# Later units' loads on ACT's queue, one-op state updates and a merged gather, in a two-layer attention kernel

## The chip, the cores and the metric

The kernel runs on one core of a Trainium2 chip. The metric is device time in microseconds (us) of one execution, the median of three runs.

## The reference

Gated linear attention over 4 batches x 8 heads, 768 tokens, head dimension 48, and behind it two feed-forward layers on the 3072 x 384 result, all in float32:

```python
state = np.zeros((B, H, D, D))
for t in range(S):
    state = alpha[:, :, t, :, None] * state + np.einsum('bhd,bhe->bhde', k[:, :, t], v[:, :, t])
    y[:, :, t] = np.einsum('bhd,bhde->bhe', q[:, :, t], state)
x = y.transpose(0, 2, 1, 3).reshape(B * S, H * D)
...
h = x @ w_in;  x = np.maximum(0.01 * h, h) @ w_out
h = x @ w2_in; out = np.where(h > 0, h, np.exp(np.minimum(h, 0)) - 1) @ w2_out
```

384 -> 2048 -> 384 in both layers. The weights are stored as 64-bit floats.

## The kernel before

**Engines.** PE is the matrix engine (TensorE), DVE the vector engine, ACT the scalar engine, POOL the general one, SP the engine that only starts transfers. A tile scheduler decides the order of the instructions on each engine and places the waits; the code gives it the order in which the steps are written. Each engine works through its own list in order. A transfer is started from the list of the engine that issues it, and that engine stops there until the transfer's conditions hold (its buffer is free; the transfer before it on the same of eight completion counters has landed).

**Attention.** The 3072 tokens are cut into 24 units of 128 tokens with all 8 heads, six units for each batch. Heads go in pairs: 112 partitions hold head 0 of a pair on 0 to 47 and head 1 on 64 to 111. For unit u, `load_unit` brings a "pack" (alpha, k and q, L113, three buffers) and `load_v` brings vt (L118, three buffers). `attn_prep` scans the decay products on DVE (E L130, F L134) and scales k and q (L136, L137). `attn_S` makes the scores sc (L149) and the transposed keys pk (L154) on PE; `attn_S_post` masks the scores into A (DVE, L161), copies pk to kn (ACT, L164) and multiplies the state S by the unit's decay into T (DVE, L169). `attn_V` adds A-by-values (L181) and T-by-queries (L186) in PSUM (po), and makes pu, the state's increment (L193). `attn_V_post` splits po into a rounded part xh (ACT, L202) and a rest xl (DVE, L203), and makes the new S = pu + T (DVE, L210; a copy in a batch's first unit, L212). T is one constant tile with zero blocks: for each head of a pair its own 48 of 96 columns are written, so T and S take one op for each half, and the matmul of L186 runs over all 112 rows.

**FFN1.** Four units make a block of 512 tokens; six blocks, each with 16 steps over 128 of the 2048 hidden columns. `gather` (L218) moves the 96 feature rows that do not fit the heads' layout with 12 transfers a block. A step is `ffn1_h` (hp, L259), `ffn1_g` (leaky ReLU, L267 on ACT and L268 on DVE; split into gh, L79 on ACT, and gl, L82 on DVE) and `ffn1_y` (L284), each product made of three passes (high x high, low x high, high x low). hp runs two steps ahead of y. The attention of block j+1 lies among the steps of block j. `next_load(u + 3)` is called at the end of unit u (L400).

**Weights.** `stage1(m)` loads step m's weights as 64-bit words into one of four slots (L418 to L420), and ACT and DVE turn them into a high and a low part (L232, L233, L241 on ACT; L237, L238, L240, L244 on DVE). This goes on during the attention of the first four units and block 0. The second layer's weights are converted the same way in FFN1's last block, from slots that `fill2` loads (L434).

**FFN2.** Six blocks of 512 tokens with 16 steps each: L313, then L320 and L321 on ACT, L322 on DVE, L79 and L82, then L344. A guard loads each unit's alpha again (span, L491) and checks its range with two ACT passes (L495, L496). It is written at every other step from block 1 on (L668).

Of the kernel before, what the change touches and what calls it, by code (L numbers as in the profile page):

```python
# [19 lines left out]
def attention_two_layers_kernel(  # L20
# [40 lines left out]

    ident = const.tile([128, 128], F32, name="ident")
    causal = const.tile([128, C], F32, name="causal")
    T = const.tile([PR, NP, PD], F32, name="T")
    d0 = const.tile([PR, EXT], F32, name="d0")
    d1 = const.tile([PR, EXT], F32, name="d1")
    bias = const.tile([PR, 2], F32, name="bias")
# [17 lines left out]
    def constants():  # L85
        make_identity(nc, ident)
        nc.gpsimd.memset(causal, 1.0)
        nc.gpsimd.affine_select(
            out=causal, in_=causal, compare_op=ALU.is_ge, fill=0.0,
            base=0, pattern=[[1, C]], channel_multiplier=-1,  # L90
        )
        nc.gpsimd.memset(T, 0.0)
        nc.vector.memset(d0, 0.0)
        nc.vector.memset(d0[:, 0:EXT:C + 1], 1.0)
        nc.vector.memset(d1, 0.0)
        nc.vector.memset(bias[:, 0:1], -1.0)
        nc.vector.memset(bias[:, 1:2], -ALPHA_SPAN)
        nc.vector.memset(far_sum[:, 1:2], 1.0)
# [3 lines left out]
    vts = {}  # L102
    st = {}

    def load_unit(u, first=False):
        t = pack_p.tile([PR, EXT + 2 * NP * C], F32, tag="pack", name="pack")
        if first:
            m = EXT + NP * C
            nc.sync.dma_start(t[:, 0:EXT], seqs[u, :, 0:EXT])
            nc.scalar.dma_start(t[:, EXT:m], seqs[u, :, EXT:m])  # L110
            nc.sync.dma_start(t[:, m:], seqs[u, :, m:])
        else:
            nc.sync.dma_start(t, seqs[u])  # L113
        packs[u] = t

    def load_v(u):
        t = v_p.tile([128, NP, 3 * D], F32, tag="v", name="vt")
        nc.sync.dma_start(t.rearrange("s p e -> s (p e)"), vals[u])  # L118
        vts[u] = t

    def ext(t, off):
# [35 lines left out]
    def attn_S_post(u):  # L157
        c = u % NC
        d = st[u]
        for j, sc in enumerate(d.pop("sc")):  # L160
            nc.vector.tensor_mul(d["A"][:, j], sc, causal.unsqueeze(1).to_broadcast([128, NP, C]))  # L161
        if c < NC - 1:
            kn = at_p.tile([128, NP, PR], F32, tag="kn", name="kn")
            nc.scalar.copy(kn, d.pop("pk"))  # L164
            d["kn"] = kn
        if c > 0:
            for j in range(2):
                r = slice(64 * j, 64 * j + D)
                nc.vector.tensor_mul(  # L169
                    T[r, :, j * D:(j + 1) * D], st["S"][r], d["pe"][r].to_broadcast([D, NP, D]))  # L170

    def attn_V(u):
        c = u % NC
        d = st[u]
        vt = vts.pop(u)
        A, qh = d["A"], d["qh"]
        po = ps_a.tile([PR, NP, C], F32, tag="at", name="po")
        for p in range(NP):
            for j in range(2):
                wide = D if j else 64  # L180
                nc.tensor.matmul(po[64 * j:64 * j + wide, p], lhsT=vt[:, p, 2 * j * D:2 * j * D + wide], rhs=A[:, j, p],  # L181
                                 start=(p == 0), stop=(p == NP - 1 and c == 0), skip_group_check=True)
        if c > 0:
            for p in range(NP):
                for j in range(2):
                    nc.tensor.matmul(po[64 * j:64 * j + D, p], lhsT=T[:, p, j * D:(j + 1) * D], rhs=qh[:, p],  # L186
                                     start=False, stop=(p == NP - 1), skip_group_check=True)
        d["po"] = po
        if c < NC - 1:
            pu = ps_a.tile([PR, NP, D], F32, tag="at", name="pu")  # L190
            for p in range(NP):
                for j in range(2):
                    nc.tensor.matmul(pu[64 * j:64 * j + D, p], lhsT=d["kn"][:, p, 64 * j:64 * j + D],  # L193
                                     rhs=vt[:, p, 2 * j * D:(2 * j + 1) * D], start=(p == 0), stop=(p == NP - 1),
                                     skip_group_check=True)
            d["pu"] = pu

    def attn_V_post(u, xh, xl, off):
        c = u % NC
        d = st.pop(u)  # L200
        po = d["po"]
        nc.scalar.copy(xh[0:PR, :, off:off + C], po)  # L202
        nc.vector.tensor_sub(xl[0:PR, :, off:off + C], po, xh[0:PR, :, off:off + C].bitcast(F32))  # L203
        if c < NC - 1:
            pu = d["pu"]
            Sn = at_p.tile([PR, NP, D], F32, tag="S", name="S")
            for j in range(2):
                r = slice(64 * j, 64 * j + D)
                if c > 0:
                    nc.vector.tensor_add(Sn[r], pu[r], T[r, :, j * D:(j + 1) * D])  # L210
                else:
                    nc.vector.tensor_copy(Sn[r], pu[r])  # L212
            st["S"] = Sn

    def gather(x, n):
        for b in range(2 * KD):
            lo, hi = 64 * (b // 3) + 16 * (b % 3), 64 * (b % 2) + D
            nc.sync.dma_start(x[hi:hi + 16, b // 2, :n].bitcast(F32), x[lo:lo + 16, KD, :n].bitcast(F32))  # L218


    w_words = [w1.bitcast(I32), w2.bitcast(I32)]
# [28 lines left out]
    steps = {}  # L250

    def ffn1_h(j, m):
        xh, xl, n = xt[j]
        hp = ps_h.tile([128, n], F32, tag="h", name="hp")
        wh, wl = win[m]
        i = 0
# [38 lines left out]
                    nc.scalar.copy(dst[:, c], ytiles[j][c])  # L295

    def x2_split(j):
        xh = xs_p.tile([128, KD, 512], F32R, tag="xh", name="xh")
        xl = xs_p.tile([128, KD, 512], F32R, tag="xl", name="xl")
        for c in range(KD):  # L300
            split(xh[:, c], xl[:, c], x2t[j][:, c], nc.scalar)
        x2s[j] = xh, xl
# [68 lines left out]
    def xtile(j):  # L371
        if j not in xt:
            n = blocks[j][1] * C
            xt[j] = (
                xs_p.tile([128, KD + 1, 512], F32R, tag="xh", name="xh"),
                xs_p.tile([128, KD + 1, 512], F32R, tag="xl", name="xl"),
                n,
            )
        return xt[j]

    def attn_pe(u, i):
# [5 lines left out]
    def attn_post(u, i):  # L387
# [4 lines left out]
                attn_prep(u + 1)  # L392
        elif i == 2:
            j = unit_block[u]
            xh, xl, _ = xtile(j)
            attn_V_post(u, xh, xl, (u - blocks[j][0]) * C)
            if u == blocks[j][0] + blocks[j][1] - 1:
                for x in (xh, xl):
                    gather(x, blocks[j][1] * C)
            next_load(u + 3)  # L400

    def next_load(u):
        if u < NU:
            load_unit(u)
            load_v(u)
        else:
            t = pack_p.tile([128, 2 * 768], I32, tag="pack", name="stg")
            slots2.extend([(t[:, 0:768], 99), (t[:, 768:1536], 99)])
# [95 lines left out]
    def general():  # L504
# [51 lines left out]
        weights(1)  # L556
        for j in range(NB):
            xt.pop(j)
            xh, xl, n = xtile(j)
            for i in range(n // C):  # L560
                r0 = blocks[j][0] * C + i * C
                xr = at_p.tile([128, KD, 128], F32, tag="A", name="xr")
# [18 lines left out]
    with ExitStack():  # L581
# [47 lines left out]
        for s, e in enumerate(seq):  # L629
# [35 lines left out]
                    conv2.b(2 * KF)  # L665
            if ph == 2 and m == 4 and (j + 1) * 512 < NT:
                x2_split(j + 1)
            if ph == 2 and j > 0:  # L668
                u, odd = divmod(after - 2 * KF, 2)
                if u <= NU and not odd:  # L670
                    if u < NU:
                        guard_load(u)
                    if u > 0:
                        guard_unit(u - 1)
                if u == NU + 1 and not odd:
                    guard()
        with tc.If(nc.values_load(near, min_val=0, max_val=1) == 0):
            general()
# [84 lines left out]
```

## Time and profile before

| | us |
|---|---|
| three runs | 987.18 to 989.9, median 989.37 |
| the profiled execution | 987.68 |
| its span, first to last instruction | 986.0 |
| busy in the span: PE / DVE / ACT | 934.5 / 545.6 / 446.6 |
| mean granted PE clock | 0.979 of full speed |

The profile is one execution recorded by the hardware profiler. Its page gives busy time by engine and the span in 40 slices; views of the same trace give stretches, groups of instructions, waits (who waited, for whom, how long in total, how often, the longest) and the instructions in order of time. PEld is PE's weight load, which overlaps its matmuls; SPq and ACTq are the transfers started from SP's and ACT's lists.

### The profile page before, as it was taken

How to read it: one execution, taken by the hardware profiler on the slowest of the kernel's cores; microseconds unless marked ns; L12 is line 12 of the kernel's file. 1: busy time of each engine (PE TensorE's matmuls, PEld its weight loads, DVE VectorE, ACT ScalarE, POOL GpSimd, SP SyncE). 2: the span in 40 equal slices, each digit the busy share in tenths (PEclk: the TensorE clock that was granted, in tenths of full speed). 3: DMA queues.
4: the chain of work that ended last, by engine and by line, in shares of the span. 5: the costliest groups of instructions: out<-in, count | busy, mean ns of one | idle time of the engine just before them, and what ended most of it. 6: DMA issues, size and time to landing. Idle time of an engine off the chain costs nothing.

```text
span 986.0 us, 13236 instructions
## 1 busy us (share of the span) xinstructions
PE 934.5 (95%) x5234; PEld 790.4 (80%) x5234; DVE 545.6 (55%) x916; ACT 446.6 (45%) x783; POOL 1.4 (0%) x9
## 2 busy tenths in 40 slices
PE   4689979899999999999999999999999999999996
PEld 3567757688788788888878889989989989899996
DVE  6799998533657556555559993433433333433332
ACT  1245453332322322233458874574574674444442
POOL 0000000000000000000000000000000000000000
PEclk9779998899999999999999999999999999999999
DMA  9655571000211212211134310030110210000001
GB/s 238 161 173 163 149 184 61 13 1 19 68 51 42 57 41 81 55 44 49 49 96 145 112 49 1 4 105 1 53 55 1 78 30 1 33 1 1 32 1 37
DMA packets 25671, 62.40 MB, mean 63 GB/s; under 512 B 4512, under 2 KB 7584, under 8 KB 25600
## 3 DMA queue, kind: packets, MB, share of 16 engines
q1 hardware_dynamic: 25472, 61.24, 22.0%
q8 instruction: 43, 0.70, 0.3%
q10 hardware_dynamic: 128, 0.23, 0.1%
q14 instruction: 28, 0.23, 0.1%
HBM read 54.37 MB, written 4.72 MB: 60 GB/s over the span
## 4 chain that ended last, share of the span: by engine, by line
PE 80%; DMA 9%; DVE 6%; ACT 2%; SPq 1%; issue 1%; DVEq 0%; ACTq 0%
PE y L284 19%; PE hp L259 18%; PE hp L313 18%; PE o L344 9%; PE oa L344 9%; DMA pack<-in_seqs_dram 3%; DMA x2t<-in_w_dram 3%; PE sc L149 2%; PE po L181 2%; DMA span<-in_seqs_dram 2%; PE po L186 1%; DMA out_dram<-osb 1%; ACT span L496 1%; DVE A L161 1%; DVE x2t L240 1%
## 5 line engine op out<-in xcount | busy, mean ns | idle before, releaser
L82 DVE TENSOR_TENSOR gl<-t,gh 128x512 fp32r<-128x512 f32 x192 | 132.1, 690 | 130.5 <-ACT gh L79 118.9
L79 ACT CAST gh<-t 128x512 fp32r<-128x512 f32 x192 | 118.9, 620 | 170.9 <-PE y L284 60.9
L284 PE MATMUL y<-gh,w 128*128 128x512 f32 x576 | 172.9, 398 | 2.9 <-ACT gh L79 2.9
L259 PE MATMUL hp<-xh,w 128*128 128x512 f32 x576 | 155.1, 402 | 4.6 <-DVE t L268 2.4
L313 PE MATMUL hp<-xh,w 128*128 128x512 f32 x576 | 149.2, 394 | 1.2 <-DVE t L322 1.2
L322 DVE SCALAR_TENSOR_TENSOR t<-t,hp 128x512 f32<-128x512 f32 x96 | 66.0, 687 | 152.2 <-ACT t L321 152.2
L259 PEld LDWEIGHTS hp<-xh,w 128*128 128x128 f32 x576 | 108.8, 192 | 29.6 <-issue 3.2
L284 PEld LDWEIGHTS y<-gh,w 128*128 128x128 f32 x576 | 107.2, 190 | 26.9 <-ACT gh L79 3.7
L313 PEld LDWEIGHTS hp<-xh,w 128*128 128x128 f32 x576 | 106.5, 188 | 19.0 <-DVE t L322 2.2
L284 PE MATMUL y<-gl,w 128*128 128x512 f32 x288 | 105.2, 399 | 0.4 <-DVE gl L82 0.4
L320 ACT ACTIVATE t<-hp 128x512 f32<-128x512 f32 x96 | 57.0, 594 | 105.8 <-PE hp L313 105.7
L268 DVE TENSOR_TENSOR t<-t,hp 128x512 f32<-128x512 f32 x96 | 65.2, 681 | 59.3 <-ACT t L267 59.1
L344 PE MATMUL oa<-w,gh 128*128 128x384 f32 x384 | 96.3, 337 | 1.3 <-ACT gh L79 1.3
L267 ACT ACTIVATE t<-hp 128x512 f32<-128x512 f32 x96 | 56.4, 596 | 90.7 <-PE hp L259 90.5
L344 PE MATMUL o<-w,gh 128*128 128x384 f32 x384 | 95.1, 337 | 1.9 <-ACT gh L79 1.9
L259 PE MATMUL hp<-xl,w 128*128 128x512 f32 x288 | 83.4, 393 | 0.0
L313 PE MATMUL hp<-xl,w 128*128 128x512 f32 x288 | 81.9, 392 | 0.0
L344 PEld LDWEIGHTS o<-w,gh 128*128 128x128 f32 x384 | 70.5, 188 | 7.7 <-ACT gh L79 2.7
L344 PEld LDWEIGHTS oa<-w,gh 128*128 128x128 f32 x384 | 70.1, 188 | 4.5 <-ACT gh L79 1.7
L284 PEld LDWEIGHTS y<-gl,w 128*128 128x128 f32 x288 | 53.6, 189 | 13.6 <-DVE gl L82 1.3
L313 PEld LDWEIGHTS hp<-xl,w 128*128 128x128 f32 x288 | 54.1, 188 | 12.2
L259 PEld LDWEIGHTS hp<-xl,w 128*128 128x128 f32 x288 | 54.3, 189 | 11.7 <-issue 0.2
(94 smaller groups left out, 1005.6 us busy)
## 6 DMA issues: line engine op xcount, KB each, us to landing
pack<-in_seqs_dram SPq DMA_DIRECT2D x23, 674.2 KB, 5.6
stg<-in_w_dram SPq DMA_DIRECT2D x28, 384.0 KB, 3.1
x2t<-in_w_dram SPq DMA_DIRECT2D x20, 384.0 KB, 4.6
vt<-in_vals_dram SPq DMA_DIRECT2D x24, 288.0 KB, 5.1
span<-in_seqs_dram SPq DMA_DIRECT2D x24, 226.2 KB, 2.7
x2t<-in_w_dram SPq DMA_DIRECT2D x32, 144.0 KB, 4.5
out_dram<-osb SPq DMA_DIRECT2D x24, 192.0 KB, 2.2
x2t<-in_w_dram SPq DMA_DIRECT2D x32, 48.0 KB, 4.3
```

The costliest lines, as they stand in the source:

```text
L79: nc.scalar.copy(dst, src)
L82: (lo_engine or nc.vector).tensor_sub(lo, src, dst.bitcast(F32))
L149: nc.tensor.matmul(sc[j][:, p], lhsT=kS[r, p, :], rhs=qh[r, p, :], start=True, stop=True)
L181: nc.tensor.matmul(po[64 * j:64 * j + wide, p], lhsT=vt[:, p, 2 * j * D:2 * j * D + wide], rhs=A[:, j, p], start=(p == 0), stop=(p == NP - ...
L259: nc.tensor.matmul(hp, lhsT=a[:, kk, :], rhs=x[:, kk, :n], start=(i == 0), stop=(i == 3 * KD - 1))
L267: nc.scalar.activation(t, hp, ACTF.Copy, scale=0.01)
L268: nc.vector.tensor_max(t, t, hp)
L284: nc.tensor.matmul(ytiles[j][c], lhsT=a[:, c * 128:(c + 1) * 128], rhs=x, start=(m == 0 and i == 0), stop=(m == KF - 1 and i == 2),)
L313: nc.tensor.matmul(hp, lhsT=a[:, kk, :], rhs=x[:, kk, :], start=(i == 0), stop=(i == 3 * KD - 1))
L320: nc.scalar.activation(t, hp, ACTF.Relu, scale=-1.0)
L322: nc.vector.scalar_tensor_tensor(out=t, in0=t, scalar=-1.0, in1=hp, op0=ALU.add, op1=ALU.max)
L344: nc.tensor.matmul(otiles[j][i], lhsT=a[:, i * 128:(i + 1) * 128], rhs=x, start=(m == 0 and n == 0), stop=(m == KF - 1 and n == 2),)
```

## The change

Four things. T becomes a tile of each unit with one 48-column block per head, written by one op over all 112 partitions, and S likewise; the T matmul runs over a head's 48 rows; POOL's memset of T goes. xh and xl of a block become two halves of one tile, and the gather moves both with 6 transfers in place of 12. The loads of units 3 to 23 are issued from ACT's list in place of SP's. The guard takes five units in each of FFN2's blocks 0 to 4, from step 6 on.

```diff
-    T = const.tile([PR, NP, PD], F32, name="T")
...
-        nc.gpsimd.memset(T, 0.0)
...
-    def load_unit(u, first=False):
+    def load_unit(u, first=False, eng=None):
...
-            nc.sync.dma_start(t, seqs[u])
+            (eng or nc.sync).dma_start(t, seqs[u])
...
-    def load_v(u):
+    def load_v(u, eng=None):
...
-        nc.sync.dma_start(t.rearrange("s p e -> s (p e)"), vals[u])
+        (eng or nc.sync).dma_start(t.rearrange("s p e -> s (p e)"), vals[u])
...
         if c > 0:
-            for j in range(2):
-                r = slice(64 * j, 64 * j + D)
-                nc.vector.tensor_mul(
-                    T[r, :, j * D:(j + 1) * D], st["S"][r], d["pe"][r].to_broadcast([D, NP, D]))
+            T = at_p.tile([PR, NP, D], F32, tag="cT", name="T")
+            nc.vector.tensor_mul(T, st["S"], d["pe"].to_broadcast([PR, NP, D]))
+            d["T"] = T
...
-                    nc.tensor.matmul(po[64 * j:64 * j + D, p], lhsT=T[:, p, j * D:(j + 1) * D], rhs=qh[:, p],
+                    r = slice(64 * j, 64 * j + D)
+                    nc.tensor.matmul(po[r, p], lhsT=d["T"][r, p], rhs=qh[r, p],
                                      start=False, stop=(p == NP - 1), skip_group_check=True)
...
-                    nc.tensor.matmul(pu[64 * j:64 * j + D, p], lhsT=d["kn"][:, p, 64 * j:64 * j + D],
+                    r = slice(64 * j, 64 * j + (D if j else 64))
+                    nc.tensor.matmul(pu[r, p], lhsT=d["kn"][:, p, r],
...
-            for j in range(2):
-                r = slice(64 * j, 64 * j + D)
-                if c > 0:
-                    nc.vector.tensor_add(Sn[r], pu[r], T[r, :, j * D:(j + 1) * D])
-                else:
-                    nc.vector.tensor_copy(Sn[r], pu[r])
+            if c > 0:
+                nc.vector.tensor_add(Sn, pu, d["T"])
+            else:
+                nc.vector.tensor_copy(Sn, pu)
...
-            nc.sync.dma_start(x[hi:hi + 16, b // 2, :n].bitcast(F32), x[lo:lo + 16, KD, :n].bitcast(F32))
+            nc.sync.dma_start(x[hi:hi + 16, :, b // 2, :n].bitcast(F32), x[lo:lo + 16, :, KD, :n].bitcast(F32))
...
-                for x in (xh, xl):
-                    gather(x, blocks[j][1] * C)
+                gather(t, blocks[j][1] * C)
             next_load(u + 3)
...
-            load_unit(u)
-            load_v(u)
+            load_unit(u, eng=nc.scalar)
+            load_v(u, eng=nc.scalar)
...
-            if ph == 2 and j > 0:
-                u, odd = divmod(after - 2 * KF, 2)
-                if u <= NU and not odd:
-                    if u < NU:
-                        guard_load(u)
-                    if u > 0:
-                        guard_unit(u - 1)
-                if u == NU + 1 and not odd:
+            if ph == 2 and m >= KF - 10 and m % 2 == 0:
+                u = 5 * j + (m - KF + 10) // 2
+                if u < NU:
+                    guard_load(u)
+                if 0 < u <= NU:
+                    guard_unit(u - 1)
+                if u == NU:
                     guard()
```

The scheduler orders each engine's list anew. Three places follow, each before and after. (The changed file is shorter, so its line numbers are lower by up to 8; buffer numbers differ as well.)

ACT's list at the start of the program, before: stage words x2t, copies kn and xh of the first units, no transfer.

```order
L233 ACTIVATE x2t_135<-x2t_135 128x768
L164 COPY kn<-pk 128x448
L233 ACTIVATE x2t_136<-x2t_136 128x768
L202 CAST xh<-po 112x4x128
L233 ACTIVATE x2t_137<-x2t_137 128x768
L164 COPY kn<-pk 128x448
L233 ACTIVATE x2t_138<-x2t_138 128x768
```

The same place after:

```order
L230 ACTIVATE x2t_134<-x2t_134 128x768
L162 COPY kn<-pk 128x448
L111 DMA pack<-in_seqs_dram 112x1541
L230 ACTIVATE x2t_135<-x2t_135 128x768
L201 CAST x<-po 112x4x128
L116 DMA vt<-in_vals_dram 128x576
L162 COPY kn<-pk 128x448
L230 ACTIVATE x2t_136<-x2t_136 128x768
L230 ACTIVATE x2t_137<-x2t_137 128x768
L116 DMA vt<-in_vals_dram 128x576
```

The pack of unit 3 stands behind the first kn copy, its vt behind the first copy of po. In SP's list the two stood behind all loads of the first four weight steps.

DVE's list around the last layer-1 weight conversion (w_15), before:

```order
L82 TENSOR_TENSOR gl<-t,gh 128x512
L244 TENSOR_TENSOR w_15_134<-x2t_140,w_15_133 128x768
L244 TENSOR_TENSOR w_14_132<-x2t_139,w_14_131 128x768
L130 SCALAR_TENSOR_TENSOR E<-pack,d_97 112x517
L132 TENSOR_SCALAR pe<-E 112x4
L136 TENSOR_TENSOR pack<-pack,E 112x512
L133 RECIPROCAL d_98<-pe 112x4
L134 SCALAR_TENSOR_TENSOR F<-pack,d_98 112x516
L137 TENSOR_TENSOR pack<-pack,F 112x512
L203 TENSOR_TENSOR xl<-po,xh 112x4x128 x3
L268 TENSOR_TENSOR t<-t,hp 128x512
```

The same place after:

```order
L81 TENSOR_TENSOR gl<-t,gh 128x512
L241 TENSOR_TENSOR w_15_133<-x2t_139,w_15_132 128x768
L265 TENSOR_TENSOR t<-t,hp 128x512
L81 TENSOR_TENSOR gl<-t,gh 128x512
L265 TENSOR_TENSOR t<-t,hp 128x512
L202 TENSOR_TENSOR x<-po,x 112x4x128 x2
L81 TENSOR_TENSOR gl<-t,gh 128x512
L265 TENSOR_TENSOR t<-t,hp 128x512
L81 TENSOR_TENSOR gl<-t,gh 128x512
L202 TENSOR_TENSOR x<-po,x 112x4x128
L265 TENSOR_TENSOR t<-t,hp 128x512
L128 SCALAR_TENSOR_TENSOR E<-pack,d_96 112x517
```

The three xl copies (x<-po after) stood behind the preparation of unit 13 (E to pack), and now stand ahead of it.

ACT's list in the first bunch of the guard, which begins FFN2's block 1, before; what lies between one gh cast (ahead of the first row) and the next:

```order
L495 ACTIVATE span<-span,bias 112x4x128
L496 ACTIVATE span,outside<-span,bias 112x4x128
L320 ACTIVATE t<-hp 128x512
L496 ACTIVATE span,outside<-span,bias 112x4x128
L495 ACTIVATE span<-span,bias 112x4x128
L321 ACTIVATE t<-t 128x512
L495 ACTIVATE span<-span,bias 112x4x128
L496 ACTIVATE span,outside<-span,bias 112x4x128
L320 ACTIVATE t<-hp 128x512
L495 ACTIVATE span<-span,bias 112x4x128
L496 ACTIVATE span,outside<-span,bias 112x4x128
L79 CAST gh<-t 128x512
```

After, the longest stretch between two gh casts in a bunch:

```order
L78 CAST gh<-t 128x512
L488 ACTIVATE span<-span,bias 112x4x128
L489 ACTIVATE span,outside<-span,bias 112x4x128
L488 ACTIVATE span<-span,bias 112x4x128
L317 ACTIVATE t<-hp 128x512
L489 ACTIVATE span,outside<-span,bias 112x4x128 x2
L318 ACTIVATE t<-t 128x512
L488 ACTIVATE span<-span,bias 112x4x128
L317 ACTIVATE t<-hp 128x512
L489 ACTIVATE span,outside<-span,bias 112x4x128
L78 CAST gh<-t 128x512
```

The guard's bunches had 8 units and stood at the start of blocks 1 to 3; now they have 5, at the starts of blocks 1 to 4 and one in block 0 beside the last weight conversions. (L495 and L496 became L488 and L489; L320 and L321 became L317 and L318.)

## Rows read from the trace of the kernel before

**Rows 1.** Stretches: length; busy us of PE, PEld, DVE, ACT, POOL; clock; DMA share; GB/s

```profile
0.00:25.00 25.00, 10.89 (x74) 8.63 (x74) 16.63 (x32) 4.21 (x6) 1.45 (x9) 1.00 0.95 238
30.00:167.00 137.00, 117.33 (x805) 90.41 (x805) 130.01 (x209) 58.80 (x87) 0.00 (x0) 0.89 0.52 144
200.00:250.00 50.00, 50.00 (x240) 41.24 (x239) 16.56 (x24) 15.21 (x25) 0.00 (x0) 1.00 0.09 22
646.00:714.00 68.00, 66.72 (x334) 59.95 (x333) 24.59 (x37) 41.09 (x77) 0.00 (x0) 1.00 0.13 38
850.00:918.00 68.00, 68.00 (x344) 61.50 (x343) 23.19 (x35) 31.15 (x52) 0.00 (x0) 1.00 0.04 12
```

**Rows 2.** Waits of DVE, 30 to 170 us (us in total, times, longest)

```profile
DVE E L130 <- DMA pack<-in_seqs_dram: 6.7, 3, 4.7
```

**Rows 3.** Waits of PE, 30 to 170 us

```profile
PE sc L149 <- DVE S L210: 3.2, 1, 3.2
...
PE hp L259 <- DMA xh<-xh: 2.1, 1, 2.1
```

**Rows 4.** DVE's groups by shape, 0 to 170 us (busy us, mean ns | idle before)

```profile
L161 DVE TENSOR_TENSOR A<-sc,causal 128x512 f32<-128x512 f32 x22 | 14.7, 680 | 0.0
...
L169 DVE TENSOR_TENSOR T<-S,pe 48x192 f32<-48x192 f32 x18 | 6.2, 347 | 0.3
...
L210 DVE TENSOR_TENSOR S<-pu,T 48x192 f32<-48x192 f32 x14 | 4.8, 346 | 1.0 <-PE pu L193 0.8
```

**Rows 5.** Timeline (start, us, instruction, idle before), 14 to 38 us, four engines

```profile
14.83 0.52 ACT L164 COPY kn<-pk 128x448 f32<-128x448 f32 x1
...
22.79 0.34 SPq L113 DMA_DIRECT2D pack<-in_seqs_dram  x1
...
29.94 0.90 ACT L232 ACTIVATE x2t<-x2t 128x768 f32<-128x768 f32 x1
...
30.46 1.24 DVE L130 TENSOR_TENSOR_SCAN E<-pack,d 112x517 f32<-112x517 f32 x1 [4.74 <-DMA pack<-in_seqs_dram]
...
37.55 0.96 DVE L238 SCALAR_TENSOR_TENSOR x2t<-x2t 128x768 int32<-128x768 int32 x1
```

**Rows 6.** The page's part 6: loads by line, KB each, us to landing

```profile
pack<-in_seqs_dram SPq DMA_DIRECT2D x23, 674.2 KB, 5.6
...
vt<-in_vals_dram SPq DMA_DIRECT2D x24, 288.0 KB, 5.1
```

**Rows 7.** Timeline, 171 to 177 us, DVE and PE

```profile
171.38 1.23 DVE L130 TENSOR_TENSOR_SCAN E<-pack,d 112x517 f32<-112x517 f32 x1 [4.26 <-DMA pack<-in_seqs_dram]
...
176.15 0.56 PE L193 MATMUL pu<-vt,kn 128*48 128x48 f32 x16 [2.88 <-DVE xl L203]
```

**Rows 8.** Waits of PE, 500 to 986 us

```profile
PE o L344 <- ACT gh L79: 1.9, 2, 1.0
PE hp L259 <- DVE t L268: 1.5, 1, 1.5
PE oa L344 <- ACT gh L79: 1.3, 1, 1.3
PE hp L313 <- DVE t L322: 1.2, 2, 0.8
```

**Rows 9.** Timeline, 269 to 271 us, ACT and SP's queue

```profile
269.67 0.58 ACT L202 CAST xh<-po 112x512 fp32r<-112x512 f32 x1 [1.65 <-PE po L181]
...
270.02 0.35 SPq L118 DMA_DIRECT2D vt<-in_vals_dram  x1
```

**Rows 10.** Stretch 200 to 300 us, PE's passes of L149, then of L186

```profile
200.00:300.00 100.00, 4.23 (x44) 3.27 (x44) 1.00 0.12 34
...
200.00:300.00 100.00, 2.29 (x32) 2.00 (x32) 1.00 0.12 34
```

**Rows 11.** Timeline, 254 to 258 us, ACT and PE

```profile
254.13 0.62 ACT L79 CAST gh<-t 128x512 fp32r<-128x512 f32 x1 [4.51 <-DVE t L268]
...
257.59 0.39 PE L284 MATMUL y<-gh,w 128*128 128x512 f32 x1
```

More of the change, by code (lines that the diff above doesn't have):

```diff
@@ L252, in ffn1_h @@
     def ffn1_h(j, m):
-        xh, xl, n = xt[j]
+        xh, xl, n, _ = xt[j]
         hp = ps_h.tile([128, n], F32, tag="h", name="hp")
@@ L297, in x2_split @@
     def x2_split(j):
-        xh = xs_p.tile([128, KD, 512], F32R, tag="xh", name="xh")
-        xl = xs_p.tile([128, KD, 512], F32R, tag="xl", name="xl")
+        t = xs_p.tile([128, 2, KD + 1, 512], F32R, tag="x", name="x")
+        xh, xl = t[:, 0], t[:, 1]
         for c in range(KD):
@@ L373, in xtile @@
             n = blocks[j][1] * C
[L374 to L378, printed above, removed]
+            t = xs_p.tile([128, 2, KD + 1, 512], F32R, tag="x", name="x")
+            xt[j] = t[:, 0], t[:, 1], n, t
         return xt[j]
@@ L394, in attn_post @@
             j = unit_block[u]
-            xh, xl, _ = xtile(j)
+            xh, xl, _, t = xtile(j)
             attn_V_post(u, xh, xl, (u - blocks[j][0]) * C)
             if u == blocks[j][0] + blocks[j][1] - 1:
-                for x in (xh, xl):
-                    gather(x, blocks[j][1] * C)
+                gather(t, blocks[j][1] * C)
             next_load(u + 3)
@@ L558, in general @@
             xt.pop(j)
-            xh, xl, n = xtile(j)
+            xh, xl, n, _ = xtile(j)
             for i in range(n // C):
```

## The prediction

> **What bounds the kernel now.** I read the stretches first. From 200 us on TensorE (PE) is busy all the time, 50.00 of 50 us, and DVE's 16.6 and ACT's 15.2 us of work lie beside it [rows 1]. FFN2 reads the same where no guard runs (68.00 of 68) and loses 1.3 us in a stretch with one (66.72). So after 200 us a faster DVE is worth nothing; only PE's own idle time can go. Earlier it is the other way round: in the 137 us from 30 to 167 DVE is busy for 130.0, PE for 117.3 and ACT for 58.8 [rows 1]. What DVE waits for around it is above all a unit's pack, 6.7 us before the decay scan, L130 [rows 2]. PE waits there for what DVE makes, 3.2 us for one S [rows 3]. So the first 170 us are as long as DVE's list of work plus its few waits, the next 400 as long as PE's matmuls, and FFN2 as long as PE's matmuls plus the guard's stalls.
>
> The granted clock of the stretch from 30 to 167 us is 0.89 on average [rows 1], so a part of it ran at the 1.2 GHz level. DVE is the bound there, so I count nothing for it; and PE's 19.7 idle us are more than what I take from DVE below.
>
> The profiled execution took 987.68 us (span 986.0). The median of the three runs, 989.37, is 1.7 us above it; I sum against the former and add 1.7.
>
> **1. T and S as one op each.** Up to 170 us DVE runs 18 T ops of 347 ns and 14 S ops of 346, each on 48 partitions x 192 [rows 4], and 4 S copies, which I take to be as long. The change makes one of two. The new op spans 112 partitions, still with 192 elements each. The mask multiply on 128 partitions takes 680 ns for 512, 1.3 ns an element; T on 48 takes 1.8 [rows 4]: more partitions don't make an element dearer, so I take a merged op to be as long as one was. 18 fewer ops x 0.35 = **6.3 us** less of DVE, all where DVE is the bound. The old ops behind 170 us lie beside PE's work: nothing.
>
> **2. Unit 3's pack.** DVE stands still for 4.74 us up to 30.46, because SP issued this load only at 22.79, behind the stage loads of four weight steps; it landed 7.7 us later [rows 5]. In the new order it stands on ACT right behind the copy of unit 0's pk, which ended at 15.35 [rows 5]. With 7.7 us to land it is there at about 23, before DVE ran dry at 25.7, and the whole 4.74 would go. But its bytes are not free. In the first 25 us the transfers are busy 0.95 of the time at 238 GB/s [rows 1]; unit 3's pack and vt, 674 + 288 KB [rows 6], set what is behind them back by 962 / 238 = 4.0 us, and that is weights of steps 2 and 3, which ACT has to have before the scale (L232) at 29.94. That ends at 30.84, and DVE's L238 needs it at 37.55 [rows 5]: 6.7 us of room, 2.0 once DVE comes 4.7 earlier. So 4.0 − 2.0 = 2.0 come back as a wait for ACT. Bounds 0 to 4.7; I take **2.7**.
>
> Here a rule speaks against the change. The Trainium skill, "DMA: Bandwidth & Descriptors", section "Issuing engines are not separate DMA queues", says that transfers started by any engine run on the same 16 DMA engines and interleave, so that starting them from several engines saves only the sequencer's time. By it this term would be 0 and the sum 2.7 smaller. The share of 0.95 agrees with it; a load that sat in SP's list while DVE was idle speaks against it.
>
> **3. The other waits for packs** up to 170 us: 6.7 − 4.7 = 2.0 us [rows 2, 5]. Bounds 0 to 2.0, I take **1.0**.
>
> **4. Unit 13's pack.** In SP's list a stage load stands ahead of it. DVE waited 4.26 us for it until 171.38, with three xl copies queued behind its preparation, and PE stood 2.88 us until 176.15 for the last of these [rows 7]. PE is the bound by then, so only the 2.88 count. In the new order the xl copies stand ahead of that scan, and even a late load doesn't hold PE. Bounds 0 to 2.9, I take **2.9**.
>
> **5. The guard.** Its waits are all of PE's idle time in FFN2: 1.9 + 1.3 us for gh, 1.2 for t [rows 8], 4.4 in all, in three bunches of 8 units that the scheduler puts at the starts of blocks 1 to 3. Now there are five bunches of 5. Between two gh casts ACT had four first and four second guard passes in the bunch shown above, and has three and four now, so the delay of a gh shrinks by one pass, and each bunch ends earlier. I leave 0.4 us for each of five: 4.4 − 2.0, rounded to **2.5**. Bounds 0 to 4.4.
>
> **6. The gather.** Six issues instead of twelve, each carrying both parts. PE waits 2.1 us for the first [rows 3], where DVE's list is the bound anyway, and the first matmul of the pass after the last waits 1.5 for a t behind the splits on DVE [rows 8]. Bounds 0 to 1.5, I take **1.0**.
>
> **7. What the change adds.** 42 loads go onto ACT's list. The issue of one took SP 0.35 us [rows 9]; 15 us in all, on an engine that is idle for over half of every stretch but FFN2's [rows 1]. An issue also waits until its buffer is free. Behind unit 8's pu SP issued the vt load at 270.02 [rows 9]; the xh copy, behind which ACT would issue it, began at 269.67 and takes 0.58 us [rows 9], so there the wait is nothing. In PE's stretch the cost is hidden if gh has room for 2 x 0.35 us, and the least that I found between the end of a gh cast and its first matmul is 2.8 us (254.75 to 257.59) [rows 11]. Up to 167 us ACT feeds DVE's conversions: 11 units x 0.7 = 7.7 us of issue on an ACT that is busy 58.8 of 137 us [rows 1]. Bounds 0 to 7.7; I take **+2.5**, nearer to 0, since ACT is idle for more than half of the time. T·qh goes from 112 to 48 rows, with the same 48 weight columns and 128 moving ones: 16 passes in each of 20 units, 11 of which lie behind 170 us: 176 passes where PE is the bound. The nearest rows are its own, 2.29 / 32 = 72 ns each, and the scores' 48-row passes, 4.23 / 44 = 96 [rows 10]; from below, two halves of a pair side by side would save 36. Bounds −6.3 to +4.2 us. I take 0, since as many columns stream. POOL's memset of T lay beside the first loads: nothing.
>
> **Sum:** −6.3 − 2.7 − 1.0 − 2.9 − 2.5 − 1.0 + 2.5 = −13.9, so 973.8 for a profiled execution, and with 1.7 more **975.5 us** for the median.
>
> **Rivals.**
> *The start gives nothing.* ACT's list is in order: a pack load that waits there holds the conversions behind it, and weights come as much later as packs come earlier. What DVE saves in terms 1 to 3 it then waits away, the issues' 2.5 with it, and terms 4 to 6 remain, −6.4: 983 (981 to 986.4). For it: the share of 0.95, and ACT's scale only at 29.94. It is the skill's rule above with ACT's order on top. Against: 130 of 137 us busy, where a removed op must show. Chance 0.17.
> *Nothing measurable*, 986.4 to 992.3 (0.3% either way is about what a measurement of this kernel can tell from no change): the first rival, and the issues at their bound of 7.7 in place of 2.5. Chance 0.08.
> *Slower: the loads hold gh.* In PE's stretch an ACT that waits for pu holds the gh cast behind it, and y on PE needs that. If the new order puts pu a step of 4.1 us behind po, each of 13 units costs 4.1 + 0.7 − 2.8 = 2.0 us, 26 in all, and with the −13.9 the time is 1001. It decides from a wait of 2.1 us per unit on, and eats the whole gain at 3.2. For it: the scheduler is free to put pu later. Against: unit 8's rows. Chance 0.12.
> Forecast, 963 to 981: chance 0.63.
>
> **How the numbers follow.** All terms at their best give −6.3 − 4.7 − 2.0 − 2.9 − 4.4 − 1.5 = −21.8, 967.6, and 961 with all of the matmuls' 6.3; I stop at 963. Upwards the range takes in the first rival and what its bounds leave, to 988. It leaves out the slower rival and most of the unchanged case, some 2 in 10. Faster by over 0.3% holds the forecast and the first rival, 0.80; same 0.08; slower 0.12.
>
> **What would show it.** Right: T and S once per unit at about 350 ns; under 2 us of idle time before unit 3's scan; DVE's last layer-1 conversion done some 8 us before 167; no wait of pu for xl at 176; FFN2's waits for gh and t at 2 us or less. Wrong: ACT waiting over a microsecond in front of a load with gh behind it; PE waiting for gh between 200 and 500 us; DVE waiting for L232 or L241 before 167; a merged op near 700 ns; T·qh passes at 96 ns.

## The result and the profile after

The changed kernel takes 971.99 us (median of four runs, 971.32 to 973.39), the kernel before 988.58 (four runs, 987.18 to 989.9). The ratio is 0.9834 with a 95% interval of 0.9815 to 0.9853, some 16.4 us faster. The forecast was 975.5, within 963 to 988. Two single executions among the experiments took far longer than the others of their kernels, 1246.96 us of the kernel before and 1848.2 us (the profiled one) of the changed kernel with 12 transfers; the times and ratios below leave both out, and the second gives no rows.

| | before | after |
|---|---|---|
| profiled execution / its span, us | 987.68 / 986.0 | 971.32 / 969.6 |
| PE / DVE / ACT busy, us | 934.5 / 545.6 / 446.6 | 929.8 / 529.4 / 445.8 |
| mean granted clock | 0.979 | 0.987 |

The stretches of the changed kernel, answering to [rows 1] (length; busy us of PE, PEld, DVE, ACT, POOL; clock; DMA share; GB/s):

```profile
30.00:167.00 137.00, 122.31 (x832) 90.89 (x828) 120.49 (x188) 62.86 (x93) 0.00 (x0) 0.93 0.52 146
646.00:714.00 68.00, 68.00 (x343) 61.58 (x342) 25.08 (x38) 38.51 (x69) 0.00 (x0) 1.00 0.09 29
850.00:918.00 68.00, 68.00 (x344) 61.72 (x343) 23.06 (x34) 31.47 (x52) 0.00 (x0) 1.00 0.04 12
```

DVE is busy for 120.5 of the 137 us that had 130.0, PE for 122.3 against 117.3, and the stretch of FFN2 with a guard is as full as the one without. The forecast lay 3.5 us above the measured time, and the sections below show that the sum was better than its terms.

**The start.** The same instructions as in [rows 5], on ACT, its queue and DVE (start, us, instruction, idle before):

```profile
14.39 0.51 ACT L162 COPY kn<-pk 128x448 f32<-128x448 f32 x1
...
15.30 0.32 ACTq L111 DMA_DIRECT2D pack<-in_seqs_dram  x1
...
24.96 1.24 DVE L128 TENSOR_TENSOR_SCAN E<-pack,d 112x517 f32<-112x517 f32 x1 [0.22 <-DMA pack<-in_seqs_dram]
...
30.93 0.90 ACT L230 ACTIVATE x2t<-x2t 128x768 int32<-128x768 uint16 x1 [3.48 <-DMA x2t<-in_w_dram]
...
31.73 0.88 ACT L229 ACTIVATE x2t<-x2t 128x768 f32<-128x768 f32 x1
...
32.63 0.96 DVE L235 SCALAR_TENSOR_TENSOR x2t<-x2t 128x768 int32<-128x768 int32 x1 [2.51 <-ACT x2t L229]
```

Unit 3's pack is issued at 15.30 in place of 22.79, and its scan waits 0.22 us in place of 4.74. Then DVE waits 2.51 us for the scale L229 (L232 before). Weights hold that up: on ACT, L230 ahead of it waits 3.48 us for a weight load. 2.0 us were expected there.

**T and S** are one op each, of the length of one of the two before [rows 4] (DVE's groups, 0 to 170 us):

```profile
L166 DVE TENSOR_TENSOR T<-S,pe 112x192 f32<-112x192 f32 x9 | 3.2, 354 | 0.0
L207 DVE TENSOR_TENSOR S<-pu,T 112x192 f32<-112x192 f32 x7 | 2.4, 343 | 0.0
```

**What DVE waits for** from 30 to 167 us (total, times, longest), against [rows 2]:

```profile
DVE E L128 <- DMA pack<-in_seqs_dram: 6.0, 4, 2.3
DVE w L241 <- ACT w L238: 2.7, 6, 1.2
DVE x2t L235 <- ACT x2t L229: 2.5, 1, 2.5
DVE t L265 <- ACT t L264: 1.9, 2, 1.8
DVE gl L81 <- ACT gh L78: 1.7, 1, 1.7
```

and in the kernel before, those for ACT:

```profile
DVE t L268 <- ACT t L267: 1.5, 2, 1.2
DVE w L244 <- ACT w L241: 0.9, 1, 0.9
```

The packs cost 6.0 us without unit 3's, where the kernel before had 2.0, and the waits for ACT have grown from 2.4 to 8.8 us. Together that is about the 9.5 us by which DVE is less busy: much of what DVE saved, it waited away.

**What PE waits for** from 70 to 480 us, in the kernel before (its three longest):

```profile
PE sc L149 <- DVE A L161: 3.0, 1, 3.0
PE y L284 <- ACT gh L79: 2.9, 3, 2.3
PE pu L193 <- DVE xl L203: 2.9, 1, 2.9
```

and in the changed kernel:

```profile
PE y L281 <- ACT gh L78: 1.6, 3, 0.7
PE hp L256 <- ACT w L238: 0.8, 1, 0.8
PE hp L256 <- DVE w L241: 0.5, 1, 0.5
```

From 480 us to the end it waits for this, against [rows 8]:

```profile
PE hp L256 <- DMA x<-x: 0.8, 2, 0.4
PE o L341 <- ACT x2t L292: 0.2, 1, 0.2
```

The long waits are gone, the one of pu for xl at 176 us [rows 7] and all of FFN2's among them. Three of the long ones, in two places, had cost twice. Stretches of the kernel before, each with the stalls and what follows them:

```profile
139.00:147.00 8.00, 2.73 (x13) 1.80 (x11) 6.76 (x11) 5.23 (x8) 0.00 (x0) 0.98 0.58 162
147.00:157.00 10.00, 9.97 (x34) 8.19 (x35) 9.65 (x16) 2.62 (x5) 0.00 (x0) 0.67 0.01 2
173.00:176.00 3.00, 0.26 (x2) 0.00 (x0) 2.93 (x5) 2.22 (x5) 0.00 (x0) 1.00 0.00 0
176.00:185.00 9.00, 8.82 (x47) 7.29 (x48) 6.98 (x14) 1.83 (x3) 0.00 (x0) 0.62 0.10 35
```

PE is busy 2.73 of 8.0 us and then runs at a granted clock of 0.67 for 10 us, busy 0.26 of 3.0 and then at 0.62 for 9. In these followers PE is full, so a part of each at the 1.2 GHz level costs 10 x 0.33 + 9 x 0.38 = 6.7 us. The changed kernel has a clock of 1.00 from 70 us to PE's last matmul.

**An account.** With every gap of PE over 0.15 us added up, and the clock's loss as length x (1 - granted clock) over stretches of 5 us, the profiled spans come apart like this (us):

| kernel | span | PE idle from 70 us on | clock's loss from 70 us on | the rest |
|---|---|---|---|---|
| before | 986.0 | 18.1 | 6.8 | 961.1 |
| after | 969.6 | 4.0 | 0.0 | 965.6 |
| joint x tile, 6 transfers | 973.0 | 8.8 | 5.1 | 959.1 |
| joint x tile, 12 transfers | 983.5 | 11.2 | 11.9 | 960.4 |
| guard alone | 984.7 | 16.5 | 6.8 | 961.4 |
| loads on ACT alone | 989.4 | 17.8 | 6.8 | 964.8 |
| after, two ops | 971.5 | 4.5 | 2.1 | 964.9 |
| after, loads on SP | 964.1 | 0.0 | 0.0 | 964.1 |

The loss is counted up to PE's last matmul; what of it falls inside a gap stands in both columns, 2.5 us with 12 transfers and under 1 us elsewhere. The rest, which holds the first 70 us, PE's work behind them and what follows its last matmul, is 963 within 4 us in every kernel. The first 70 us, with all that the change does there, hardly tell kernels apart; PE's stalls behind 70 us, and the slow clock that some of them bring, do. The change took 20.9 us of these away, and its rest is 4.5 us longer, so that 16.4 remain. In a second profile of the changed kernel (span 968.1, stalls 4.8, no loss) the rest is 963.3, so differences of 2 to 3 us in it are scatter.

### The profile page after: what moved, and what is told of

Read it like the earlier page. It is cut to its first block, busy times and chain, and to the rows that moved or that the text cites. A ratio compares the mean times of both kernels' runs of the same rounds, so it can differ in the third digit from the quotient of the medians.

```text
span 969.6 us, 13094 instructions
## 1 busy us (share of the span) xinstructions
PE 929.8 (96%) x5234; PEld 781.8 (81%) x5234; DVE 529.4 (55%) x876; ACT 445.8 (46%) x783; POOL 1.1 (0%) x8
## 4 chain that ended last, share of the span: by engine, by line
PE 79%; DVE 8%; DMA 8%; ACT 2%; issue 1%; SPq 1%; DVEq 0%; ACTq 0%
PE hp L310 20%; PE hp L256 16%; PE y L281 15%; PE o L341 10%; PE oa L341 10%; DMA x2t<-in_w_dram 3%; DMA pack<-in_seqs_dram 2%; PE po L178 2%; DMA stg<-in_w_dram 2%; PE sc L147 2%; PE po L184 2%; DMA x<-x 1%; DVE x2t L235 1%; DVE t L265 1%; DVE gl L81 1%
## 5 line engine op out<-in xcount | busy, mean ns | idle before, releaser
L256 PE MATMUL hp<-x,w 128*128 128x512 f32 x864 | 218.6, 395 | 4.1 <-DMA x<-x 2.7
L310 PE MATMUL hp<-x,w 128*128 128x512 f32 x864 | 215.4, 393 | 0.0
L256 PEld LDWEIGHTS hp<-x,w 128*128 128x128 f32 x864 | 160.4, 188 | 41.2 <-issue 3.2
L310 PEld LDWEIGHTS hp<-x,w 128*128 128x128 f32 x864 | 160.7, 188 | 29.3
L317 ACT ACTIVATE t<-hp 128x512 f32<-128x512 f32 x96 | 57.1, 595 | 103.7 <-PE hp L310 103.6
L341 PE MATMUL oa<-w,gl 128*128 128x384 f32 x192 | 63.0, 337 | 0.0
L318 ACT ACTIVATE t<-t 128x512 f32<-128x512 f32 x96 | 60.8, 633 | 2.3
L341 PE MATMUL o<-w,gl 128*128 128x384 f32 x192 | 61.0, 336 | 0.0
L147 PEld LDWEIGHTS sc<-pack 48*128 48x128 f32 x384 | 32.0, 210 | 20.3 <-issue 9.3
```

The source lines that it names most:

```text
L147: nc.tensor.matmul(sc[j][:, p], lhsT=kS[r, p, :], rhs=qh[r, p, :], start=True, stop=True)
L256: nc.tensor.matmul(hp, lhsT=a[:, kk, :], rhs=x[:, kk, :n], start=(i == 0), stop=(i == 3 * KD - 1))
L310: nc.tensor.matmul(hp, lhsT=a[:, kk, :], rhs=x[:, kk, :], start=(i == 0), stop=(i == 3 * KD - 1))
L317: nc.scalar.activation(t, hp, ACTF.Relu, scale=-1.0)
L318: nc.scalar.activation(t, t, ACTF.Exp, scale=-1.0)
L341: nc.tensor.matmul(otiles[j][i], lhsT=a[:, i * 128:(i + 1) * 128], rhs=x, start=(m == 0 and n == 0), stop=(m == KF - 1 and n == 2),)
```

## Experiments

The ratios below are to runs of the kernel before on the same chip; that kernel's median was between 988.6 and 991.5 us there, so kernels that were not measured side by side are compared by ratio. "The changed kernel" stands at 0.9834 (0.9815 to 0.9853) and, measured again beside three of the versions below, at 0.9813 (0.9795 to 0.9832).

### The loads back on SP

```diff
-            load_unit(u, eng=nc.scalar)
-            load_v(u, eng=nc.scalar)
+            load_unit(u)
+            load_v(u)
```

> The changed kernel with one part undone: the loads of units 3 to 23 go back to SP's list. By the prediction's terms 2 to 4 and the issues (2.7 + 1.0 + 2.9 - 2.5) the time rises by 4.1 us, to 976, and DVE again stands idle for more than 3 us before unit 3's decay scan. By the rival that only the order of the same bytes changes (a transfer costs the same whoever issues it), the time stays at 972 within 2 us. If the loads carry most of the gain, it rises by 8 us or more, to 980.

966.35 us, ratio 0.9755 (0.9724 to 0.9786): faster than the changed kernel, which no expectation had. So it ran again, beside the changed kernel:

> The changed kernel with its unit loads back on SP's list, once more. If that is really faster, its time is again 5 to 6 us below the changed kernel's; if the earlier difference came from the chip, the two agree within 2 us.

> The changed kernel once more, on the chip and in the rounds of the next three, so that they can be compared directly: 0.983 of the time of the kernel before, as at first.

965.61 us, 0.9731 (0.9713 to 0.9749), against 972.16 us, 0.9813. The loads on ACT cost 6.5 us by the medians, 8 by the ratios. The stretch from 70 to 200 us with the loads on SP:

```profile
70.00:200.00 130.00, 130.00 (x774) 98.88 (x774) 104.74 (x161) 61.76 (x97) 0.00 (x0) 1.00 0.41 110
```

and in the changed kernel:

```profile
70.00:200.00 130.00, 126.83 (x769) 95.97 (x768) 105.54 (x164) 60.45 (x94) 0.00 (x0) 1.00 0.38 107
```

With the loads on SP, PE has not one gap there, although unit 3's scan waits for its pack again, as in the kernel before:

```profile
29.72 1.24 DVE L128 TENSOR_TENSOR_SCAN E<-pack,d 112x517 f32<-112x517 f32 x1 [4.12 <-DMA pack<-in_seqs_dram]
```

The scheduler's list for DVE tells the difference: ahead of the last layer-1 conversion it has 11 units' preparations and 208 instructions, in the changed kernel 13 and 224. With packs planned to come earlier, units are prepared earlier, and conversions, which FFN1's steps wait for, come later: the last one ends at 155.5 us against 162.9 (160.0 in the changed kernel's second profile). In line with that, 1.3 us of PE's waits in the changed kernel (the list from 70 to 480 us above) are for converted weights, w of L238 and L241. But the end of the last conversion does not rank kernels by itself: in the kernel with the joint tile and 6 transfers (further down) it comes at 173.0 us, later than the 167.1 of the kernel before, and that kernel is 17 us faster.

### The loads on POOL's list

```diff
-            load_unit(u, eng=nc.scalar)
-            load_v(u, eng=nc.scalar)
+            load_unit(u, eng=nc.gpsimd)
+            load_v(u, eng=nc.gpsimd)
```

> The changed kernel with the unit loads on POOL's list, which is empty by then. DVE's list has 224 instructions ahead of the last layer-1 conversion and 13 units prepared there, as in the changed kernel, against 208 and 11 with the loads on SP. If loads on ACT cost time because they hold the conversions and gh casts behind them in ACT's list, this is as fast as with SP, 966 or less. If the cost is that units are prepared earlier, ahead of conversions, it stays near 972.

969.8 us, 0.9777 (0.976 to 0.9794), between the two: 2.4 us faster than on ACT, 4.2 slower than on SP (3.6 and 4.6 by the ratios). DVE's list has the same 13 preparations and 224 instructions as with ACT, so I put the 4.2 us down to what is prepared when, and the 2.4 to loads that stand in ACT's list. That is argued from the counts, not shown: whether a transfer that POOL starts has a price of its own was not tried apart. It may have one: by the profiles' pages a pack lands 5.5 us after its issue from POOL's list and a vt 5.3, against 4.8 and 3.0 from ACT's and 5.2 and 4.7 from SP's. PE's waits from 70 to 480 us:

```profile
PE y L281 <- ACT gh L78: 1.3, 2, 1.0
PE hp L256 <- ACT w L238: 0.8, 2, 0.6
```

They are of the same kinds as in the changed kernel and about as long, so this split is by the times, not by these rows. The account does not show it either: behind 70 us this profile has 2.4 us of stalls and 3.4 of slow clock, 1.8 more in all than the slower changed kernel.

### Two ops for T and S

```diff
-            nc.vector.tensor_mul(T, st["S"], d["pe"].to_broadcast([PR, NP, D]))
+            for j in range(2):
+                r = slice(64 * j, 64 * j + D)
+                nc.vector.tensor_mul(T[r], st["S"][r], d["pe"][r].to_broadcast([D, NP, D]))
...
-            if c > 0:
-                nc.vector.tensor_add(Sn, pu, d["T"])
-            else:
-                nc.vector.tensor_copy(Sn, pu)
+            for j in range(2):
+                r = slice(64 * j, 64 * j + D)
+                if c > 0:
+                    nc.vector.tensor_add(Sn[r], pu[r], d["T"][r])
+                else:
+                    nc.vector.tensor_copy(Sn[r], pu[r])
```

> The changed kernel with T and S written by two ops of 48 partitions each, in the unit's own T tile; the matmul keeps its 48 rows. By term 1 (18 more DVE ops of 0.35 us where DVE is the bound) the time rises by 6.3 us, to 978. If DVE's list is not what sets the end of block 0 (it waits for weights and packs anyway), the time stays within 1.5 us of 972.

973.53 us, 0.9829 (0.9802 to 0.9857): 1.5 us by the medians, by the ratios nothing against 0.9834 and 1.6 against 0.9813, and not 6.3. The stretch from 30 to 167 us:

```profile
30.00:167.00 137.00, 119.40 (x791) 90.68 (x788) 126.11 (x201) 61.24 (x90) 0.00 (x0) 0.86 0.52 146
```

and DVE's longest waits in it:

```profile
DVE w L245 <- ACT w L242: 3.5, 5, 1.6
DVE E L128 <- DMA pack<-in_seqs_dram: 3.0, 3, 1.9
DVE x2t L239 <- ACT x2t L233: 2.2, 2, 1.8
```

DVE is busy for 126.1 us in place of 120.5, and waits less: 3.0 us for packs in place of 6.0, and none of the 1.9 for t. All its waits in the stretch come to 10.1 us in place of 14.8. Most of the time of the added ops lay where DVE would have waited.

### One op, joint tile, nothing else

The changed kernel with three parts undone, the loads, the guard's places (as further down) and the transfers of the gather:

```diff
-            load_unit(u, eng=nc.scalar)
-            load_v(u, eng=nc.scalar)
+            load_unit(u)
+            load_v(u)
...
-            if ph == 2 and m >= KF - 10 and m % 2 == 0:
+            if ph == 2 and j > 0:
...
+            for h in range(2):
+                nc.sync.dma_start(x[hi:hi + 16, h, b // 2, :n].bitcast(F32), x[lo:lo + 16, h, KD, :n].bitcast(F32))
```

> The changed kernel without the moved loads, the guard's new places and the 6-transfer gather: what is left is T and S as one op, the 48-row T matmul and the joint x tile. By term 1, 6.3 us faster than before. By the run with two ops (1.5 us slower than the changed kernel), 1.5 us faster.

978.72 us, 0.9888 (0.9855 to 0.992). This is 11 us faster than before, more than either expectation. But it contains the joint x tile, and that alone gives the same (0.9889, two experiments on): T and S as one op and the 48-row matmul add nothing that can be seen, within some 4 us that the two intervals leave.

### The joint tile with 6 and with 12 transfers

The kernel before with this part of the change:

```diff
-            xt[j] = (
-                xs_p.tile([128, KD + 1, 512], F32R, tag="xh", name="xh"),
-                xs_p.tile([128, KD + 1, 512], F32R, tag="xl", name="xl"),
-                n,
-            )
+            t = xs_p.tile([128, 2, KD + 1, 512], F32R, tag="x", name="x")
+            xt[j] = t[:, 0], t[:, 1], n, t
...
-            nc.sync.dma_start(x[hi:hi + 16, b // 2, :n].bitcast(F32), x[lo:lo + 16, KD, :n].bitcast(F32))
+            nc.sync.dma_start(x[hi:hi + 16, :, b // 2, :n].bitcast(F32), x[lo:lo + 16, :, KD, :n].bitcast(F32))
```

> The kernel before with one part of the change: both parts of x in one tile and a gather of 6 transfers. Undoing this in the changed kernel (12 transfers) cost about 7 us. If the parts add, this is 7 us faster than before. By term 6 it is 1.0 us faster. If what counts is where the scheduler puts units' preparations against the weight conversions, the two directions need not agree, and DVE's count of preparations ahead of the last conversion tells which way it goes: fewer than in the kernel before, faster.

973.77 us, 0.9831 (0.9802 to 0.9861): by itself as much as the whole change. DVE has as many preparations (13) and instructions (242) ahead of the last conversion as before, so that count is not how. What went are stalls: FFN2's and the one at 506 us [rows 8] are all gone, although the guard stands where it stood, and of the long ones before 200 us one is left, 3.0 us for gh:

```profile
PE y L284 <- ACT gh L79: 4.1, 3, 3.0
PE po L181 <- issue: 1.4, 1, 1.4
```

The same joint tile with 12 transfers:

```diff
+            for h in range(2):
+                nc.sync.dma_start(x[hi:hi + 16, h, b // 2, :n].bitcast(F32), x[lo:lo + 16, h, KD, :n].bitcast(F32))
```

> The kernel before with both parts of x in one tile and still 12 transfers in the gather. With 6 transfers this was 16.7 us faster than before. If the number of transfers gives the gain, nearly all of it is lost, and the time is within 4 us of before. If the joint tile gives it, by way of the order that the scheduler then finds (12 units prepared ahead of the last conversion in place of 13, 233 DVE instructions in place of 242), it stays 13 us or more faster than before.

981.5 us, 0.9889 (0.9863 to 0.9916): neither of the two expected. By the ratios the tile gives 11 us and the halved number of transfers another 5 to 6. SP's queue in the first gather of the two kernels, with 12 and with 6 transfers:

```profile
53.45 9.37 SPq L219 DMA_DIRECT2D x<-x  x12
```

```profile
56.36 3.95 SPq L218 DMA_DIRECT2D x<-x  x6
```

12 hold SP's list for 9.4 us and 6 for 4.0. With 12 a unit's vt and then weights stand behind them; with 6 the vt stands ahead. Yet the first weight load behind the gather starts at 63.58 us with 12 and at 62.40 with 6, only 1.2 us apart, and DVE's list differs too (12 preparations ahead of the last conversion in place of 13). So the time is shown to go with the number of transfers, but not that SP's list is the way. The stalls of the 12-transfer kernel, each with the stretch behind it:

```profile
98.00:102.00 4.00, 0.18 (x1) 0.21 (x2) 3.67 (x7) 0.90 (x2) 0.00 (x0) 0.62 0.57 187
102.00:110.00 8.00, 8.00 (x25) 6.43 (x26) 7.94 (x15) 4.14 (x6) 0.00 (x0) 0.55 0.00 0
125.00:128.00 3.00, 0.25 (x1) 0.25 (x2) 2.31 (x4) 2.27 (x5) 0.00 (x0) 0.72 0.83 226
128.00:135.00 7.00, 7.00 (x33) 5.33 (x34) 7.00 (x11) 5.34 (x8) 0.00 (x0) 0.63 0.62 179
172.00:175.00 3.00, 0.45 (x3) 0.28 (x2) 2.93 (x5) 1.47 (x4) 0.00 (x0) 0.85 0.00 0
175.00:185.00 10.00, 10.00 (x39) 7.70 (x40) 4.54 (x8) 3.29 (x6) 0.00 (x0) 0.70 0.00 0
```

PE stands almost still three times, and each time the clock is between 0.55 and 0.70 over the stretch that follows. The account's 11.9 us are these, 9.2 in the stretches that follow and the rest in the stalls themselves.

In the changed kernel, back to 12 transfers:

> The changed kernel with 12 transfers a block in the gather, one tile for both parts kept. By term 6 the time rises by 1.0 us, to 973. If the longer gather on SP's list holds back the weights behind it in block 0, where DVE waits for them, it rises by 3 us or more; if neither, no change within 1 us.

978.5 us (median of six), 0.9877 (0.985 to 0.9903): 4 to 6.5 us, the largest of the three expectations, and the same size as on the kernel before. Without rows it does not show whether weights were held back, as that expectation had it.

### The guard

The old places in the changed kernel:

```diff
-            if ph == 2 and m >= KF - 10 and m % 2 == 0:
-                u = 5 * j + (m - KF + 10) // 2
...
+            if ph == 2 and j > 0:
+                u, odd = divmod(after - 2 * KF, 2)
```

> The changed kernel with the guard at every other step from FFN2's block 1 on, as before. PE's list up to FFN2 is the same. By term 5 the time rises by 2.5 us (at most 4.4), to 974.5, with PE waits for gh and t of 3 to 4.4 us in FFN2. If FFN2's waits were hidden by something else, the time stays at 972 within 1 us.

971.55 us, 0.9823 (0.9793 to 0.9852): no difference, and not because the bunches do nothing. ACT and PE around one gh cast of the first bunch:

```profile
641.53 0.60 ACT L78 CAST gh<-t 128x512 fp32r<-128x512 f32 x1
...
642.19 0.97 PE L341 MATMUL oa<-w,gh 128*128 128x384 f32 x4
```

The cast ends at 642.13 and its first matmul starts at 642.19. The bunch uses up all the room, but this time just no more than that: PE has no wait from 480 us on.

The new places in the kernel before:

```diff
-            if ph == 2 and j > 0:
-                u, odd = divmod(after - 2 * KF, 2)
...
+            if ph == 2 and m >= KF - 10 and m % 2 == 0:
+                u = 5 * j + (m - KF + 10) // 2
```

> The kernel before with the guard's new places alone; all lists are the same up to FFN1's last block. By term 5 it is 2.5 us faster (at most 4.4), with PE waits in FFN2 of 2 us or less. By the run that put the old places back into the changed kernel (no difference), nothing within 1 us, with waits of PE for gh and t still near 4 us.

984.84 us, 0.9934 (0.9913 to 0.9956), 6.5 us faster. PE's waits from 480 us on, against [rows 8]:

```profile
PE hp L259 <- DVE t L268: 1.5, 1, 1.5
PE hp L313 <- DVE t L322: 0.9, 1, 0.9
```

Of the 4.4 us in FFN2 0.9 are left, 3.5 saved. The interval, 4.4 to 8.6 us, lies above that: some 1 us or more of the gain has no stall of FFN2 that accounts for it, and in this one profile the stalls ahead of FFN2 are even 1.9 us longer than before. So term 5 was right about FFN2's stalls in the kernel before, but in the changed one they do not come back with the old places; with the joint tile alone they were gone as well.

### The loads on ACT alone

The kernel before, with an argument for the issuer in both load functions:

```diff
-            load_unit(u)
-            load_v(u)
+            load_unit(u, eng=nc.scalar)
+            load_v(u, eng=nc.scalar)
```

> The kernel before with the loads of units 3 to 23 on ACT's list alone. By terms 2 to 4 and the issues, 4.1 us faster than before. If the parts add as undoing them showed (loads back on SP made the changed kernel 5.6 us faster), it is 5 us slower than before. In both cases unit 3's scan starts some 5 us earlier than at 30.5.

988.04 us, 0.9956 (0.9933 to 0.9979): 4.4 us faster by the ratio, 3.4 by the medians; its profiled execution, 991.21 us with a span of 989.4, is the slowest of its twelve. Unit 3's scan starts at 26.3 us. Here the loads help and in the changed kernel they hurt: the parts do not add. Alone, they come to 11.1 (one op and joint tile), 5.7 (6 transfers), 6.5 (guard) and 4.4 us (loads), 27.7 together, where the change gives 16.4.

## Why the forecast was right, and where its terms were not

**Bound by DVE up to 170 us: half right.** DVE was busy for 130 of 137 us, and I took each op removed as time gained. The step that failed is "all where DVE is the bound". Undoing the op count cost 1.5 us, and beside the joint tile it gave nothing that shows: a list that is 95% full and has waits for ACT and for loads in it gave a removed op back as a wait. Term 1 was 6.3 us and measured 0 to 1.5.

**Term 2, unit 3's pack**, went as it was worked out: 4.74 us of idle time down to 0.22, 2.5 of it back as a wait for the scale on ACT, 2.0 us net on DVE in place of 2.7. That it shortens the kernel no run shows: with the loads back on SP the scan waits 4.12 us again, and the kernel is faster. **Term 3** had the wrong sign: waits for other packs rose from 2.0 to 6.0 us.

**Term 4** had the right stall and half its price. The 2.88 us are gone, and so are 3.4 us of slow clock behind them (9 us at 0.62). I had counted nothing for the clock, since DVE was the bound; behind 140 us it no longer was. And the moved loads are not needed for it: the stall is gone too with the joint tile and all loads on SP.

**Term 5**, 2.5 us, is 3.5 in the kernel before and 0 in the changed one.

**Term 6** was the worst: 1.0 us for a part that gives 4 to 6.5 with its number of transfers, and in the kernel before 11 with its tile. I priced the wait of the first matmul behind a gather. The joint tile's new order of all lists I did not price at all, nor 12 issues that hold SP's list for 9.4 us against 4.0, of which the runs leave open what they cost.

**Term 7**, 2.5 us for the loads on ACT's list, can't be had apart from what terms 2 to 4 gain: together they were to gain 4.1 us, and cost 6.5. By the run on POOL's list 2.4 of these go with ACT's list itself; the other 4.2 I put, as argued above, on the order that earlier loads lead the scheduler to, which was in no term. T·qh did not change, as taken, 3.25 / 48 = 68 ns a pass against 72 [rows 10] (stretch 200 to 300 us, this line alone):

```profile
200.00:300.00 100.00, 3.25 (x48) 2.48 (x48) 1.00 0.17 47
```

The errors cancelled, and that the sum came within 3.5 us was luck. In the changed kernel, terms 1 and 5 promised 8.8 us and gave 0 to 1.5, and the loads (terms 2, 3, 4 and 7) promised 4.1 and cost 6.5; against these, some 18 us too much, stand the joint tile and the halved transfers, which gave 16 to 17 us in the kernel before where term 6 had 1.0. The parts do not add, so this is no exact sum. Two of the prediction's signs also went against it: DVE waited for the scale (2.5 us) and for ACT's part of w (2.7 us) before 167 us, which it had listed as a sign of being wrong, and the last conversion was done 4 us before 167, not 8. The rule that I weighed, the Trainium skill's "DMA: Bandwidth & Descriptors", section "Issuing engines are not separate DMA queues", says that issuing from several engines saves only the sequencer's time; the runs go further, since in the changed kernel SP's own list is the best place, by 4.2 us over an idle POOL's and 6.5 over ACT's. The first rival saw that the start would give little: the first conversion ended 8.6 us earlier than before (36.6 against 45.2), the last 4.2 (162.9 against 167.1). The slower rival did not come: from 200 to 480 us PE waits for nothing.

**Left open:** why the joint tile leads the scheduler to an order with fewer stalls, how the number of transfers acts, what in the order of the lists costs the 4.2 us, and whether the account's rest, 959 to 966, has a cause or is scatter.

**A version that beats both** is the changed kernel with its loads on SP: 965.61 us, 0.9731 of the time before.

## What to carry to other kernels

In a kernel whose order a scheduler finds, a part's price by its own instructions is a weak guide, and parts do not add; undo each one from the finished version, as the loads here, before keeping it. Don't price a group of transfers by the wait of its first reader alone: that said 1.0 us here, and halving their number gave 4 to 6.5. Price a stall of PE where PE is the bound with the slow clock that can follow it. Loads that come earlier are not a gain by themselves: here unit 3's scan ran 4.8 us earlier with them (24.96 against 29.72), and the kernel took 6.5 us longer. The likely reason, argued and not shown, is that work that nobody waits for then runs ahead of work that somebody does.

## What the runs showed of the hardware

A stall's second price was the surprise. Behind PE stalls of 2.6 to 4.2 us (at 98, 125 and 172 us with 12 transfers, at 173 us before) the granted clock fell, for 2.6 to 3.6 us of loss each in the stretch that follows. Shorter stalls were followed by it too. In the kernel with the loads on ACT alone PE stood for 2.0 us in FFN2, and the clock fell right behind (the stretch with the stall, and the one behind it):

```profile
658.00:660.00 2.00, 0.08 (x1) 0.00 (x0) 0.00 (x0) 2.00 (x6) 0.00 (x0) 1.00 0.45 116
660.00:664.00 4.00, 3.96 (x13) 3.94 (x14) 1.98 (x3) 4.00 (x9) 0.00 (x0) 0.57 0.00 0
```

It is not so behind each. Behind the 1.5 us at 507 us in the kernel before [rows 8] the clock stayed at 1.00, and in the changed kernel's second profile PE stood for 2.2 us near the last gather, and the clock stayed as well:

```profile
487.00:489.00 2.00, 0.00 (x0) 0.01 (x1) 0.00 (x0) 1.33 (x3) 0.00 (x0) 1.00 0.34 67
489.00:500.00 11.00, 10.91 (x46) 8.73 (x47) 10.16 (x19) 8.23 (x17) 0.00 (x0) 1.00 0.19 58
```

So in these runs a stall's length alone does not tell whether the clock falls behind it.

Up to 70 us the granted clock differed between two profiles of the same kernel with no trace in the time: its loss there was 10.2 us in the changed kernel's first profile (971.32 us) and 20.5 in its second, whose span is 1.5 us shorter.
